# A ConvNeXt block on one core: normalised rows on three of every four partitions, read in three transfers

## The chip, the cores and the metric

The kernel runs on one core of a Trainium2 chip. A core has TensorE (PE; its weight loads are shown as PEld), VectorE (DVE), ScalarE (ACT), GpSimd (POOL) and SyncE (SP), which here issues transfers and does no arithmetic, and 16 DMA engines that all queues share. SyncE's transfers go through one hardware queue, GpSimd's through a software queue. The metric is the device time of one execution in microseconds (us).

## The reference

The input is one image of 512 x 512 pixels with 96 channels in bf16. The block is a depthwise 3 x 3 convolution, a layer norm over the channels, a linear layer from 96 to 384, gelu, a global response norm, a linear layer back to 96 and a residual:

```python
    for i in range(K):
        for j in range(K):
            out = out + xp[:, i:i+H, j:j+W, :] * dw[i, j][None, None, None, :]
    h = _layernorm(out, axis=-1)
    h = jnp.einsum('bhwc,ce->bhwe', h, w1)
    h = _gelu(h)
    gx = jnp.sqrt((h * h).sum(axis=(1, 2), keepdims=True) + 1e-6)
    nx = gx / (gx.mean(axis=-1, keepdims=True) + 1e-6)
    h = grn_gamma * (h * nx) + grn_beta + h
    h = jnp.einsum('bhwe,ec->bhwc', h, w2)
    return x + h
```

The response norm needs, for each of the 384 hidden channels, the sum of squares of gelu's output over the whole image. No pixel of the output can be made before the last pixel of h has been summed. So the work falls into two phases.

## The kernel before

The image is cut into 128 blocks of 4 rows (2,048 pixels). **Phase 1** goes through slots, one block of convolution in each. A block's input is loaded by SyncE (`load_x`, tile xin), turned by DVE so that channels lie on partitions (`turn_x`, xT), convolved on PE as matmuls with diagonal weights, and copied to SBUF by ACT (y_bf). A partition of y_bf holds one channel of one image row: partition 32r + c has row r and channels 3c, 3c+1, 3c+2 of the kernel's own order in its three sections. GpSimd squares it (`stage_sq`, ysq), PE sums y and ysq over the channels (`stage_stats`), and the statistics of a batch of four blocks become 1/std on GpSimd (`stage_rstd`, `stage_newton`). These are transposed by DVE (rt), written to DRAM by SyncE (`stage_rows`, r_dram) and read back as a broadcast over 32 partitions in four transfers (`stage_bcast`, tile rbc). GpSimd multiplies y by it (`stage_norm`, tile yn). The mean is taken off by the weights: w1p is w1 minus its mean over the channels.

The layout of yn is not what the linear layer needs (all 96 channels on partitions, for all 2,048 pixels of a block). So `stage_write` writes yn to DRAM in four transfers of 32 partitions (96 KB each), into `yn_dram[block]`, 96 rows of 2,048 pixels, 4 KB a row, and `stage_read` reads the 96 rows back into one of the six tiles of `yn_ring` (ynT). Row k goes to partition k. Partitions 96 to 127 of each ring tile are set to zero once, and so are rows 96 to 127 of w1p, so matmuls contract over 128 partitions.

Two slots after the read, `mlp_units` (or `mlp_tail` in the last 14 blocks) multiplies ynT by w1p on PE, ACT applies gelu (tile g), and sums of squares are taken either by DVE (bn_stats, bst) or by PE (matmuls of g with itself). For blocks whose number ends in 0, 3 or 7 ("whole"), up to the last 14, g is stored to g_dram in three parts.

All of phase 1 is in program order on each engine; the order in which the functions are called is the order in each queue. In a slot SyncE's queue holds: the next x block, the ynT read, the four writes of yn, the four broadcasts or the two transfers of rows where it is their turn in the batch, and one part of a g store. The read of a block waits for that block's write, issued one slot earlier. GpSimd's queue holds in a slot: the newton steps, yn, ysq, the rstd steps.

**Phase 2** goes over the 128 blocks in ORDER. 35 whole blocks are loaded from g_dram by GpSimd's queue (tile gl, 1.5 MB each); five blocks are still held in SBUF; for the other 88 g is made again from yn (tile gr): `load_rest` reads the block's rows into a ring tile five blocks ahead, except for the three blocks in KEPT, whose tiles are still there. This read takes 128 rows, the block's 96 and the first 32 of the next block, 512 KB; the 32 extra rows meet the zero rows of w1p. For every block, x is loaded a second time (`load_xr`, xr), GpSimd adds a bias to it (xb), PE multiplies g by the scaled w2, DVE adds xb to the result (o_sb, four buffers), and SyncE stores it (`stage_out`) after the next block's matmuls have been queued. A tile of o_sb is free again once its store has landed.

Setup: w1 is loaded by ACT's queue in three transfers of 32 rows, to partitions i, i+3, i+6 and so on, so that its rows have the order of yn_dram's. `setup_mlp` sums w1 over the channels with a matmul by ones (cen) and forms w1p. `setup_ynt` clears the ring's padding on GpSimd in the first slot.

Most calls go through a helper that records the program order, so L35 is the line of most instructions.

Of the kernel before, what the change touches and what calls it, by code (L numbers as in the profile page):

```python
# [12 lines left out]
GR = 4  # L13
# [43 lines left out]
def kernel(  # L57
# [11 lines left out]
    f32 = mybir.dt.float32  # L69
    i32 = mybir.dt.int32  # L70
    bf16 = x.dtype
    assert bf16 == mybir.dt.bfloat16

    B, H, W, C = x.shape
    E = w1.shape[1]
    assert B == 1 and dw.shape[0] == 3 and dw.shape[1] == 3
    assert C == 96 and E % 128 == 0 and W == 512
    NI = C // 32
# [8 lines left out]
    yn_dram = dram.tile([NBLK, C, GR * W], bf16, name="yn_dram")  # L87
# [6 lines left out]
    def is_held(q):  # L94
        return q in HELD

    def is_whole(q):
        return q < TAIL0 and q % 10 in WHOLE
# [11 lines left out]
    def chans(i):  # L110
        return slice(i, 64, 2) if i < 2 else slice(64, 96)
# [8 lines left out]
        return flat_ap.rearrange("p (g r m) -> p g r m", r=GR, m=MB)  # L120

    def yn_src(q):
        return yn_dram[q].rearrange("c (r w) -> c r w", r=GR)

    def yn_rows(q):
        return yn_dram[q:q + 2].rearrange("q c (r w) -> (q c) r w", r=GR)[0:128]

    def yn_dst(q, r):
        return yn_dram[q].rearrange("(c i) (r w) -> r c i w", i=NI, r=GR)[r]
# [1 line left out]
    consts = ctx.enter_context(tc.tile_pool(name="consts", bufs=1))  # L131
# [4 lines left out]
    dwx = consts.tile([9, NI, GR, 32], bf16, name="dwx")  # L136
    eye32 = consts.tile([128, 32], bf16, name="eye32")
    rowsel = consts.tile([128, GR], bf16, name="rowsel")
    w1_raw = consts.tile([C, E], bf16, name="w1_raw")
    w1p = consts.tile([128, E], bf16, name="w1p")  # L140
    Wq = consts.tile([128, NI, 3, GR, 32], bf16, name="Wq")
    w2_sb = consts.tile([128, NCH, C], bf16, name="w2_sb")
# [41 lines left out]
    with ExitStack() as p1:  # L184
        pe, dve, act, pool, sp = (InOrder(tc, e) for e in (nc.tensor, nc.vector, nc.scalar, nc.gpsimd, nc.sync))
# [3 lines left out]
        def banks(n):  # L189
            if n == 2:  # L190
                return PS[:, 0:2, :]
            ones[0] += 1
            return PS[:, 2 + ones[0] % 2:3 + ones[0] % 2, :]
# [48 lines left out]
        for b in range(min(2, NBLK)):  # L242
# [3 lines left out]
                       in_=zrow[:, None, :NI * GR * 32].to_broadcast([128, 3, NI * GR * 32]), func=ACTF.Identity)  # L246
# [4 lines left out]
        for q in range(GR):  # L251
            dve.tensor_copy(out=eye32[32 * q:32 * q + 32, :], in_=ident_f[32 * q:32 * q + 32, 32 * q:32 * q + 32])

        cen = consts.tile([C, 128], bf16, name="cen")
        xtpool = pc.enter_context(tc.tile_pool(name="xt", side="right", bufs=1))
        ypool = pc.enter_context(tc.tile_pool(name="ybf", side="right", bufs=13))
        ysqpool = pc.enter_context(tc.tile_pool(name="ysq", side="right", bufs=3))
# [25 lines left out]
        def load_rest(n, sq, pq):  # L283
            q = ORDER[n]
            v = grp.setdefault(q, {})
            if is_held(q):
                v["g"] = gs[q]
            elif is_whole(q):
                v["g"] = late.gl.tile([128, NQ, NCH, QW], bf16, name="gl")
                pq.dma_start(out=v["g"][:].rearrange("p t j w -> p (t j w)"), in_=g_dram[whole.index(q)])  # L290
            else:
                ynt = yn_ring[SLOTS[nth_made[q] % NYT]]
                if q not in KEPT:
                    sq.dma_start(out=ynt[:], in_=yn_rows(q))
                v["ynt"] = ynt

        def recompute(q, t):
# [87 lines left out]
        for j in range(GR):  # L385
            pool.memset(rowsel[32 * j:32 * j + 32, j:j + 1], 1.0)
        pool.memset(cen[:], 1.0)
        pool.memset(w1p[C:128, :], 0.0)
        dve.memset(SG, 0.0)
        busy(FILL[0])  # L390
        Ud = banks(2)[:, 0, :NI * 9].rearrange("p (i k) -> p i k", i=NI)
# [4 lines left out]
        for i in range(NI):  # L396
            dve.tensor_tensor(out=Wd[:, i], in0=eye32[:, None, :].to_broadcast([128, 9, 32]),
                              in1=Ud[:, i, :, None].to_broadcast([128, 9, 32]), op=ALU.mult)
# [13 lines left out]
                            pool.tensor_copy(out=o, in_=i_)  # L412

        for i in range(NI):
            act.dma_start(out=w1_raw[i:C:NI, :], in_=w1[chans(i), :])
        act.dma_start(out=w2_sb[:], in_=w2.rearrange("(j p) c -> p j c", p=128))
        with nc.allow_non_contiguous_dma("tiny gamma/beta load"):
            act.dma_start(out=gam_bf[:], in_=grn_gamma.rearrange("(j p) -> p j", p=128))
# [1 line left out]

        def setup_ynt():
            for t in yn_ring:
                pool.memset(t[C:128, :, :].rearrange("p r w -> p (r w)").bitcast(f32), 0.0)

        def setup_mlp():
            Us = banks(1)[:, 0, :]
            w1m, b2_ps = Us[:, :E], Us[:, E:E + C]
            pe.matmul(w1m, lhsT=cen[:], rhs=w1_raw[:], start=True, stop=True)
            for j in range(NCH):
                pe.matmul(b2_ps, lhsT=bet_bf[:, j:j + 1].to_broadcast([128, 128]), rhs=w2_sb[:, j, :],  # L430
                          start=(j == 0), stop=(j == NCH - 1))
            dve.scalar_tensor_tensor(out=w1p[:C, :], in0=w1m[:C], scalar=-1.0 / C, in1=w1_raw[:],
                                     op0=ALU.mult, op1=ALU.add)
            dve.tensor_copy(out=B2bc_f[:], in_=b2_ps)

# [210 lines left out]

        def stage_read(b):
            t = yn_ring[b % NYT]
            sp.dma_start(out=t[:C], in_=yn_src(b))
            ynts[b] = t  # L650

        bsts = {}
# [173 lines left out]
        for s in range(last_slot + 1):  # L826
# [3 lines left out]
            for b in get("read"):  # L830
                stage_read(b)
# [53 lines left out]
            else:  # L885
                b = mlp[0]
# [38 lines left out]
            if s == 0:  # L925
                setup_ynt()
            if s == 3:
                setup_mlp()
# [18 lines left out]
            if s == last_slot:  # L947
                for n in range(PRE):
                    load_rest(n, sp, sp)
# [19 lines left out]
        r = gi[:].bitcast(f32)  # L969
        for it in range(3):  # L970
# [5 lines left out]
            r = rn_[:]  # L976
# [21 lines left out]
    with p2:  # L998
        def out_part(q, o_sb, sub):
            r0 = q * GR  # L1000
            nc.sync.dma_start(
                out=out[0, r0:r0 + GR].rearrange("r w c -> (r w) c").rearrange(
                    "(p g) c -> p g c", g=PXP)[:, sub * GPS:(sub + 1) * GPS],
                in_=o_sb[:, sub * GPS:(sub + 1) * GPS])

        held = None
        FIRST = 8
        for n, q in enumerate(ORDER):
            sq, pq = (sp, pool) if n < FIRST else (nc.sync, nc.gpsimd)
            if n + PRE < NBLK:  # L1010
                load_rest(n + PRE, sq, pq)
                load_xr(n + PRE, pq)
            if 3 <= n + 2 < NBLK:
                stage_xb(ORDER[n + 2], pq, B2c)
            if n == NBLK - 1:
                stage_out(*held)
                held = None
            o_sb = stage_mm2(n, q)
            if held:
                stage_out(*held)  # L1020
            held = (q, o_sb)
# [30 lines left out]
```

## Time and profile before

| | |
|---|---|
| runs | 1481.22 us median of 3 (1476.22 to 1484.95) |
| profiled execution | span 1480.8 us; no other time of this execution is given |
| PE busy | 1391.3 us (94%) |
| ACT busy | 1414.4 us (96%) |
| POOL busy | 1300.3 us (88%) |
| DVE busy | 1182.0 us (80%) |
| granted TensorE clock | 0.994 |
| moved by DMA | 433.08 MB, 292 GB/s over the span |
| ynT reads, phase 1 | 128 of 384 KB |
| ynT reads, phase 2 | 85 of 512 KB |

The page gives busy time by engine, a strip of 40 slices, the DMA queues, the chain of work that ended last, the costliest groups of instructions with what ended the idle time before them, and the DMA issues. Further views give the same by stretch of time, the waits by pair of engines, and the timeline of one engine. "SPq" is SyncE's queue; its issues are not counted as busy time. In a timeline line the first number is the start from the span's beginning, the second the duration of the merged instructions, xN how many were merged, and the bracket is idle time before them and what ended it.

### The profile page before, as it was taken

The numbers are of one execution on the slowest core, as the hardware profiler recorded it, in microseconds if no ns is written. First come the engines' busy times: TensorE is split into PE (matmuls) and PEld (weight loads), VectorE is DVE, ScalarE is ACT, GpSimd is POOL, SyncE is SP. The second block draws the span as 40 slices with busy tenths as digits, with TensorE's granted clock in tenths as the row PEclk, the third lists the DMA queues.
The fourth block names the chain that finished last, engine by engine and source line by source line (L and its number), as shares of the span: only waits on it lengthen the run. The fifth ranks groups of instructions, "written<-read, shape, count | busy, mean of one in ns | idle before, by whom it ended". The sixth has DMA issues, their size and how long they took to land.

```text
span 1480.8 us, 54225 instructions
## 1 busy us (share of the span) xinstructions
PE 1391.3 (94%) x23125; PEld 810.4 (55%) x23125; DVE 1182.0 (80%) x2135; ACT 1414.4 (96%) x1595; POOL 1300.3 (88%) x922
## 2 busy tenths in 40 slices
PE   8888999999999999999999997789999999999998
PEld 3434444444444444444444445467777777776776
DVE  7849989999999999999999987965555555555555
ACT  7888989999999999999999999999999999999997
POOL 3459889998998999998999987569999999999997
PEclk9999999999999999999999999999999999999999
DMA  5568788788888888888888866669999999999997
GB/s 180 179 205 255 241 253 280 228 271 260 260 248 264 258 264 255 276 253 254 263 258 266 263 216 195 195 225 409 366 359 402 417 416 413 419 410 417 411 412 282
DMA packets 167768, 433.08 MB, mean 292 GB/s; under 512 B 31558, under 2 KB 81318, under 8 KB 163046
## 3 DMA queue, kind: packets, MB, share of 16 engines
q1 hardware_dynamic: 151284, 326.04, 66.3%
q0 software_dynamic: 14880, 103.43, 17.6%
q8 instruction: 181, 2.97, 0.8%
q14 instruction: 61, 0.50, 0.1%
q10 hardware_dynamic: 1362, 0.15, 0.1%
HBM read 273.30 MB, written 156.22 MB: 290 GB/s over the span
## 4 chain that ended last, share of the span: by engine, by line
PE 30%; ACT 24%; DMA 19%; POOL 13%; DVE 6%; issue 4%; SPq 4%; POOLq 0%; ACTq 0%; DVEq 0%
PE PS L35 30%; ACT g L35 16%; DMA out_dram<-o_sb 9%; POOL yn L35 6%; ACT y_bf L35 5%; POOL ysq L35 5%; SPq L35 4%; DMA yn_dram<-yn 3%; DVE bst L35 3%; DMA xin<-in_x_dram 2%; DMA rbc<-r_dram 2%; DMA ynT<-yn_dram 1%; DMA g_dram<-g 1%; DVE o_sb L35 1%; ACT xT L35 1%
## 5 line engine op out<-in xcount | busy, mean ns | idle before, releaser
L35 ACT ACTIVATE g<-PS 128x512 bf16<-128x512 f32 (+2 forms) x1062 | 727.7, 864 | 16.5 <-PE PS L35 15.6
L35 DVE BATCH_NORM_STATS2 bst<-g 128x6 f32<-128x512 bf16 x1110 | 671.3, 672 | 35.4 <-ACT g L35 34.5
L35 PE MATMUL PS<-ynT,w1p 128*128 128x512 bf16 x2181 | 609.6, 381 | 23.6 <-ACT g L35 5.4
L35 ACT ACTIVATE gr<-PS 128x1536 bf16<-128x1536 f32 x360 | 498.5, 1459 | 18.8 <-PE PS L35 13.8
L35 POOL TENSOR_TENSOR yn<-y_bf,rbc 128x1536 bf16<-128x1536 bf16 x126 | 391.3, 3108 | 77.3 <-ACT rbc L35 21.9
L35 DVE TENSOR_TENSOR o_sb<-PS,xb 128x384 bf16<-128x384 f32 x512 | 277.3, 556 | 227.0 <-PE PS L35 190.1
L324 POOL TENSOR_TENSOR xb<-xr,B2c 128x1536 f32<-128x1536 bf16 x118 | 368.1, 3133 | 4.3 <-DVE o_sb L35 2.0
L35 PE MATMUL PS<-xT,Wq 64*32 64x511 bf16 (+1 forms) x9198 | 340.5, 389 | 26.2 <-ACT y_bf L35 8.1
L35 POOL TENSOR_TENSOR ysq<-y_bf 128x1536 bf16<-128x1536 bf16 x114 | 313.6, 2752 | 12.8 <-ACT y_bf L35 12.8
L35 PEld LDWEIGHTS <-w1p 128*128 128x128 bf16 x2181 | 171.6, 98 | 222.0 <-issue 133.4
L35 PEld LDWEIGHTS <-gr 128*128 128x128 bf16 x4296 | 212.1, 98 | 68.9 <-issue 12.0
L35 PE MATMUL PS<-W2s,gr 128*128 128x96 bf16 x4224 | 223.5, 206 | 8.2 <-DVE o_sb L35 8.0
L35 PEld LDWEIGHTS <-Wq 64*32 64x32 bf16 x9216 | 111.9, 90 | 193.3 <-issue 145.9
L35 ACT ACTIVATE y_bf<-PS 128x1536 bf16<-128x1536 f32 (+2 forms) x135 | 199.4, 1482 | 17.4 <-PE PS L35 13.3
L35 DVE STREAM_TRANSPOSE xT<-xin 128x576 f32<-128x576 f32 (+1 forms) x256 | 181.4, 748 | 8.1 <-DMA xin<-in_x_dram 8.1
L35 PEld LDWEIGHTS <-g 128*128 128x128 bf16 x1704 | 104.9, 98 | 86.3 <-issue 54.3
L35 PE MATMUL PS<-w1p,ynT 128*128 128x256 bf16 (+2 forms) x822 | 125.8, 273 | 8.0 <-ACT xT L35 3.2
L35 PE MATMUL PS<-g 128*128 128x128 bf16 x1464 | 122.6, 220 | 2.9 <-DVE PS L35 2.6
L35 PEld LDWEIGHTS <-gl 128*128 128x128 bf16 x1680 | 82.8, 98 | 26.8 <-issue 5.0
L35 PE MATMUL PS<-W2s,gl 128*128 128x96 bf16 x1680 | 89.5, 206 | 3.4 <-DVE o_sb L35 3.2
L35 PEld LDWEIGHTS <-ynT 128*128 128x128 bf16 x822 | 64.1, 97 | 31.5 <-issue 13.7
L279 POOL DMA_DIRECT2D xr<-in_x_dram x115 | 63.7, 555 | 14.2 <-POOL xb L324 14.2
(105 smaller groups left out, 576.5 us busy)
## 6 DMA issues: line engine op xcount, KB each, us to landing
xin<-in_x_dram SPq DMA_DIRECT2D x126, 432.0 KB
g_dram<-g SPq DMA_DIRECT2D x105, 512.0 KB
gl<-g_dram POOLq DMA_DIRECT2D x35, 1536.0 KB, 11.3
yn_dram<-yn SPq DMA_DIRECT2D x512, 96.0 KB
ynT<-yn_dram SPq DMA_DIRECT2D x128, 384.0 KB
out_dram<-o_sb SPq DMA_DIRECT2D x127, 384.0 KB
xr<-in_x_dram POOLq DMA_DIRECT2D x123, 384.0 KB, 6.9
ynT<-yn_dram SPq DMA_DIRECT2D x85, 512.0 KB
```

What stands on the lines that cost most here:

```text
L35: r = f(*a, **k)
L279: pq.dma_start(out=xr[:], in_=x[0, r0:r0 + GR].rearrange("r w c -> (r w) c").rearrange("(p g) c -> p g c", g=PXP))
L324: pq.tensor_tensor(out=xb[:], in0=grp[q]["xr"][:], in1=bias[:, None, :].to_broadcast([128, PXP, C]), op=ALU.add)
```

## The change

Row 3c+i of a block's 96 rows goes to partition 4c+i, for c from 0 to 31 and i from 0 to 2. Every fourth partition (3, 7, 11 and so on to 127) holds zeros. This needs three transfers for each read, one for each i: 32 rows that lie 12 KB apart in DRAM, to partitions i, i+4, i+8 and so on, 128 KB each. Both phases read this way, on the same queue and at the same place in the program as the one transfer before. Phase 2 reads the 96 rows of its block alone. w1 is loaded to the same partitions, w1_raw, cen and w1p take all 128 partitions, and the memsets clear whole tiles: w1_raw in place of the last 32 rows of w1p, and the six ring tiles over 128 partitions instead of 32. The writes of yn are as before.

```diff
     def yn_src(q):
-        return yn_dram[q].rearrange("c (r w) -> c r w", r=GR)
-
-    def yn_rows(q):
-        return yn_dram[q:q + 2].rearrange("q c (r w) -> (q c) r w", r=GR)[0:128]
+        return yn_dram[q].rearrange("(c i) (r w) -> i c r w", i=NI, r=GR)
+
+    def read_yn(eng, t, q):
+        for i in range(NI):
+            eng.dma_start(out=t[i:128:4], in_=yn_src(q)[i])
...
-    w1_raw = consts.tile([C, E], bf16, name="w1_raw")
+    w1_raw = consts.tile([128, E], bf16, name="w1_raw")
...
-        cen = consts.tile([C, 128], bf16, name="cen")
+        cen = consts.tile([128, 128], bf16, name="cen")
...
                 if q not in KEPT:
-                    sq.dma_start(out=ynt[:], in_=yn_rows(q))
+                    read_yn(sq, ynt, q)
...
-        pool.memset(w1p[C:128, :], 0.0)
+        pool.memset(w1_raw[:], 0.0)
...
-            act.dma_start(out=w1_raw[i:C:NI, :], in_=w1[chans(i), :])
+            act.dma_start(out=w1_raw[i:128:4, :], in_=w1[chans(i), :])
...
-                pool.memset(t[C:128, :, :].rearrange("p r w -> p (r w)").bitcast(f32), 0.0)
+                pool.memset(t[:].rearrange("p r w -> p (r w)").bitcast(f32), 0.0)
...
-            dve.scalar_tensor_tensor(out=w1p[:C, :], in0=w1m[:C], scalar=-1.0 / C, in1=w1_raw[:],
+            dve.scalar_tensor_tensor(out=w1p[:], in0=w1m, scalar=-1.0 / C, in1=w1_raw[:],
                                      op0=ALU.mult, op1=ALU.add)
...
         def stage_read(b):
             t = yn_ring[b % NYT]
-            sp.dma_start(out=t[:C], in_=yn_src(b))
+            read_yn(sp, t, b)
             ynts[b] = t
```

## The prediction

> **What bounds the kernel now.** I read the busy time by stretch first, because the program has two phases with different limits: phase 1 runs to about 900 us, and phase 2 from about 1000 us.
>
> ```profile
> core 0: us, PE busy (x) PEld busy (x) DVE busy (x) ACT busy (x) POOL busy (x), PEclk, DMA share, GB/s
> 400.00:500.00 100.00, 95.87 (x1753) 47.05 (x1738) 99.55 (x171) 99.44 (x143) 93.38 (x71) 1.00 0.82 250
> ...
> 1050.00:1100.00 50.00, 50.00 (x740) 37.33 (x739) 28.34 (x53) 49.47 (x37) 47.12 (x29) 1.00 0.98 363
> 1100.00:1150.00 50.00, 50.00 (x735) 37.19 (x732) 28.38 (x53) 49.52 (x37) 48.38 (x30) 1.00 1.00 388
> ...
> 1200.00:1250.00 50.00, 48.19 (x704) 35.55 (x703) 26.95 (x51) 47.47 (x35) 48.37 (x31) 1.00 1.02 416
> ```
>
> The columns are the stretch, each engine's busy time and instructions, the granted clock (full throughout), the DMA share and rate. Phase 1 is ACT at 99%, and POOL's 93% hides little slack, as shown below. Phase 2 has two regimes. Up to 1142 us PE is never idle, at 363 to 388 GB/s. After that the DMA engines are full (1.02 at 411 to 417 GB/s) and PE does 708 matmuls per 50 us (mean of the six windows from 1150 to 1450) where it did 737. The waits of 1150 to 1450 say through what:
>
> ```profile
> DVE o_sb L35 <- DMA out_dram<-o_sb: 29.8, 20, 2.7
> ...
> PE PS L35 <- DVE o_sb L35: 9.3, 11, 1.6
> ```
>
> Stores land too late to free one of the four o_sb buffers, DVE stands, then PE. Second, SyncE's queue and POOL in one batch of phase 1 (timeline; start, duration):
>
> ```profile
> 405.03 2.49 SPq L35 DMA_DIRECT2D yn_dram<-yn  x4
> 407.56 1.17 SPq L35 DMA_DIRECT2D r_dram<-rt  x2
> 408.83 0.41 SPq L35 DMA_DIRECT2D g_dram<-g  x1
> 409.29 0.43 SPq L35 DMA_DIRECT2D xin<-in_x_dram  x1
> 409.90 0.59 SPq L35 DMA_DIRECT2D ynT<-yn_dram  x1
> 410.80 3.27 SPq L35 DMA_DIRECT2D yn_dram<-yn  x4
> 414.11 2.32 SPq L35 DMA_DIRECT2D rbc<-r_dram  x4
> ```
> ```profile
> 401.89 3.11 POOL L35 TENSOR_TENSOR yn<-y_bf,rbc 128x1536 bf16<-128x1536 bf16 x1
> ...
> 416.49 2.76 POOL L35 TENSOR_TENSOR ysq<-y_bf 128x1536 bf16<-128x1536 bf16 x1
> 419.88 3.11 POOL L35 TENSOR_TENSOR yn<-y_bf,rbc 128x1536 bf16<-128x1536 bf16 x1 [0.63 <-DMA xin<-in_x_dram]
> ```
>
> Here is a loop. POOL ends a yn at 405.0; SyncE at once issues its write, then rows, store, x, the ynT read, the next write and the rbc broadcast, nearly without a gap, until 416.4. The broadcast lands some 3.4 us later, and POOL, which has gone through ysq, yn, ysq, yn, ysq, stands 0.63 us for it. In 20 of the 26 batches from 200 us on, POOL has such a wait at this place (0.4 to 5.9 us). Does POOL's delay reach the end? It does through ysq, which PE needs for the sums. The slack from a ysq's end to PE's use of it (two timelines, matched block by block from block 127 back) is 5.4 us at block 34, 3.7 at 46, 1.0 at 54 and 0.06 at blocks 70, 74, 82, 98 and 126, where PE stands:
>
> ```profile
> 693.47 0.46 PE L35 MATMUL PS<-rowsel,ysq 128*128 128x4 bf16 x12 [2.01 <-POOL ysq L35]
> ```
>
> So from about block 54 POOL, ACT and SyncE's chain go at one pace (28.15 us for a batch of four), and a longer chain is paid for.
>
> **The change part by part.**
>
> *Phase 2 reads 384 KB, not 512 KB.* 85 reads save 128 KB each, 11.1 MB; 50 of them lie between 1150 and 1450, where they are 6.6 MB of 124 MB (413.8 GB/s x 300 us). What can be won is the stall: PE at 737 per 50 us would need 288 us for that stretch, 12 us less; 1.5 us (PE's idle time at 1000 to 1050) come on top. So the bounds are 0 and 13.5 us. At full pace the stretch would need 117.5 MB in 288 us, 408 GB/s: above the 388 that ran without a stall, below the 414 moved when saturated. That is on the edge, so some bursts will still stall; I take 8 us. Below nothing: two more issues ahead of each store delay it by up to 1.2 us, but the read is issued 1.1 us or more before the store's own data is ready (SyncE waited 339.6 us for DVE's o_sb in 127 waits), so I bound that loss at 3 us.
>
> *One read becomes three issues on SyncE.* The price of one more issue: a ynT read after an idle moment takes 0.325 us (median). The nearest row in shape is the w1 load: 32 rows to every third partition, back to back.
>
> ```profile
> L35 ACTq DMA_DIRECT2D w_raw<-in_w_dram x3: 593/594/602, 5.6 to 6.9; - x3
> ```
>
> The broadcast's issues, 32 rows of 4 KB, took 0.50 to 0.58 in most batches. I take 0.55, so 1.1 us per block; bounds 2 x 0.32 and 2 x 0.6. Only the first of the three can wait for the write's landing, a wait that exists already. Queued behind them on SyncE are the next write, the rows and the broadcast. In the loop above one read lies between POOL's yn and the broadcast, so rbc lands 1.1 us later; mostly the write follows its read at once (0.04 to 0.07 us), in six batches 0.25 to 0.8 us of idle time takes part of it, 0.1 on the mean. With 20 of 26 batches paying the full 1.0 and the others about 0.3: 0.8 us of POOL per batch. POOL's slack now falls by 0.6 us per batch (5.4 to 0.06 over nine); at 1.4 it is gone four batches after block 34, at block 50. The 19 batches from there to 126 pay 0.8 each, **15 us**. Bounds: 0.35 per batch (cheap issues, and the gain of the next part) is 7 us; for above see the rivals.
>
> *Rows over all 128 partitions in phase 1.* The 4 KB packets of the trace have a median of 159 ns in both phases, but a mean of 199 from 200 to 800 us against 161 from 1150 to 1450, where the reads already fill 128 partitions. If the 96-row reads cause it, six packets per engine lose 40 ns each: at most 0.24 us of a landing. Nothing waits for that read: it is issued 10 to 15 us ahead of its matmul. I count zero, and use the 0.24 in the low bound only.
>
> *The ramp.* Between 83 and 118 us the chain runs through SyncE and POOL with two reads in it (89.16, 96.63): 2 us; bounds 0 and 4.
>
> *Semaphores, memsets, w1.* Two more completions per read and engine, 9 ns each in the trace: 18 ns x 85 = 1.5 us of DMA time over phase 2, inside the edge above. The memsets go over 128 partitions with the same length per partition (six of 0.95 us, done at 12.2; the first read comes at 25.8). The w1_raw memset stands where w1p's did (over at 2.8; w1 is loaded from 5.6). The weight sum's matmul (0.33 us, once) takes 128 rows for 96. All zero; without that cover the memsets would cost 6 us once. Phase 1's matmuls have a contraction of 128 already.
>
> *Sum* against the profiled span: 1480.8 + 15 + 2 - 8 = **1490 us**. The median of the runs, 1481.22, stands 0.4 above that span, so I add nothing around it.
>
> [...]
>
> **The rivals.**
>
> *A, the other side: the issues are hidden.* SyncE idles 173 of the 600 us. If the two issues cost 0.32 each and rbc lands sooner by 0.24, the 0.35 left per batch may find POOL's small waits shrinking elsewhere; decisive is that POOL's slack at blocks 50 to 126 stays above zero. Then phase 2's gain decides: with all of PE's 10.9 us of idle time (9.4 + 1.5) gone and the ramp's 2, **1472**. Against it: the zeros at 70 to 126.
>
> *B, SyncE becomes the bound of phase 1.* From 200 to 800 it has 427 us of issues and 82.8 of landing waits; 84 blocks x 1.1 make it 602 of 600. If it enters the batch late, a second set lies in the loop: 1.9 per batch, slack gone at block 42, 21 batches x 1.7 = 36 us: 1480.8 + 36 + 2 - 8 = **1511**. For it: in the three quick blocks of a batch POOL makes a yn every 5.8 us. Against it: POOL's pause of 10 us before the next batch lets SyncE catch up.
>
> *C, phase 2 wins nothing* (the reads give way to the other loads and the stores stay late, or three small transfers drain worse): **1498**.
>
> **How the numbers follow.** Chances: forecast 0.5, A 0.2, B 0.13, C 0.17. The forecast's own range is 1482 to 1498 (phase 1 at its low bound of 7 us at one end, nothing won in phase 2 at the other). The 8-in-10 range reaches from A to just short of B: 1472 to 1508. A change within 0.5% (1473.8 to 1488.6) can hardly be told from none. Faster: two thirds of A, 0.14. Same: the rest of A and the forecast's low two fifths, 0.27. Slower: 0.59.
>
> **What would show it.** Right: the ynT reads of phase 1 as groups of three at 0.5 to 0.6 us; longer POOL waits ahead of yn; more PE waits for ysq; ACT below 99% from 500 to 900; phase 1 longer by 15 us; in phase 2 PE nearer 737 per 50 us and DVE's wait for out_dram well under 35 us. Wrong: issues of 0.3 us, unchanged POOL waits (A); SyncE busy with hardly a wait (B); DVE's wait for out_dram unchanged (C).

## The result and the profile after

The changed kernel takes 1542.15 us in the median (1533.4 to 1547.18), the kernel before 1481.83 us. The ratio is 1.0417, with a 95% interval of 1.0385 to 1.0449. The forecast was 1490 us, in a range of 1472 to 1508: right in direction, far too small in size. The profiled execution is the shortest of the changed kernel's, with a span of 1531.6 us. So the traces account for 50.8 us (1531.6 - 1480.8) of some 60.

Where they lie is read from three moments: the start of the last y_bf (the last convolution's copy), the start of the first o_sb (phase 2 begins) and of the last o_sb. The tile's view has first and last start, before and changed:

```profile
L35 DVE TENSOR_TENSOR o_sb<-PS,xb x512: 545/557/559, 975.5 to 1477.4; 128x384 bf16<-128x384 f32 x171
```
```profile
L35 DVE TENSOR_TENSOR o_sb<-PS,xb x512: 547/558/559, 1031.0 to 1528.3; 128x384 bf16<-128x384 f32 x171
```

| | before | changed | difference |
|---|---|---|---|
| last y_bf | 883.7 | 928.8 | +45.1 |
| first o_sb | 975.5 | 1031.0 | +55.5 |
| first to last o_sb | 501.9 | 497.3 | -4.6 |

Phase 2 became shorter, by about half of what was forecast. All of the loss lies in phase 1: 45 us while blocks are convolved, and 10 us behind the last convolution, where the queue still carries reads and writes of yn and PE waits 8.3 us for ynT. The busy time by stretch shows both sides (columns as in the profile before: stretch, engines with their instructions, clock, DMA share, GB/s):

```profile
400.00:500.00 100.00, 91.31 (x1637) 44.66 (x1636) 93.73 (x161) 94.35 (x135) 87.94 (x63) 0.98 0.77 245
...
1250.00:1300.00 50.00, 49.24 (x720) 36.37 (x717) 27.65 (x51) 48.64 (x37) 48.38 (x29) 1.00 1.01 398
1300.00:1350.00 50.00, 49.20 (x720) 36.33 (x718) 27.60 (x51) 48.51 (x36) 48.67 (x31) 1.00 1.01 393
```

In phase 1 every engine that computes is less busy: ACT 94 us of 100 for 99, POOL 88 for 93, and DMA has a lower share, 0.77 for 0.82. The granted clock is lower too, 0.98 for 1.00; more on it below. Something that is not on this list holds them. SyncE's queue in one batch (timeline: start, duration, merged issues) shows what, beside GpSimd:

```profile
635.13 0.39 SPq L35 DMA_DIRECT2D xin<-in_x_dram  x1
636.14 1.77 SPq L35 DMA_DIRECT2D ynT<-yn_dram  x3
637.95 3.37 SPq L35 DMA_DIRECT2D yn_dram<-yn  x4
641.42 1.17 SPq L35 DMA_DIRECT2D r_dram<-rt  x2
642.70 0.41 SPq L35 DMA_DIRECT2D g_dram<-g  x1
643.15 0.43 SPq L35 DMA_DIRECT2D xin<-in_x_dram  x1
643.76 1.89 SPq L35 DMA_DIRECT2D ynT<-yn_dram  x3
645.70 3.05 SPq L35 DMA_DIRECT2D yn_dram<-yn  x4
648.79 1.99 SPq L35 DMA_DIRECT2D rbc<-r_dram  x4
```
```profile
633.44 3.10 POOL L35 TENSOR_TENSOR yn<-y_bf,rbc 128x1536 bf16<-128x1536 bf16 x1
...
639.20 3.10 POOL L35 TENSOR_TENSOR yn<-y_bf,rbc 128x1536 bf16<-128x1536 bf16 x1
...
653.32 3.11 POOL L35 TENSOR_TENSOR yn<-y_bf,rbc 128x1536 bf16<-128x1536 bf16 x1 [2.53 <-DMA rbc<-r_dram]
```

The first yn is done at 636.5 and its write starts at 637.95; the second is done at 642.3 and its write starts 3.4 us later, at 645.70. In the batch shown of before, the second write started as soon as its yn was done, at 410.80:

```profile
407.67 3.10 POOL L35 TENSOR_TENSOR yn<-y_bf,rbc 128x1536 bf16<-128x1536 bf16 x1
```

SyncE is hardly anywhere ahead of GpSimd now: its waits for yn from 200 to 800 us were 38.0 us in 24 times before and are now (SyncE's own waits)

```profile
SPq L35 <- POOL yn L35: 1.0, 2, 0.5
```

In these 600 us SyncE's issues take 510 us (the sum of their own times), for 417 before, while fewer blocks pass: 238 read issues in threes, 79 blocks, for 84. Its pauses of more than 0.3 us between two issues shrink from 144 us to 44. The lateness goes where the prediction followed it. GpSimd waits for rbc, its ysq comes late, and PE stands. The first line is before, from 200 to 800 us, the second the changed kernel in the same stretch:

```profile
PE PS L35 <- POOL ysq L35: 3.4, 3, 2.0
```
```profile
PE PS L35 <- POOL ysq L35: 25.1, 15, 3.2
```

Behind this wait the trace has one more step, which the prediction had at nothing. One such wait, and the stretch that follows (columns as above):

```profile
517.93 0.48 PE L35 MATMUL PS<-rowsel,ysq 128*128 128x4 bf16 x12 [2.58 <-POOL ysq L35]
```
```profile
517.40:524.20 6.80, 6.04 (x68) 1.73 (x69) 4.94 (x9) 2.38 (x4) 6.80 (x4) 0.50 0.71 208
524.20:530.00 5.80, 5.57 (x106) 2.91 (x112) 5.49 (x11) 5.74 (x9) 5.20 (x2) 1.00 0.83 259
```

The granted clock is 0.50 for 6.8 us. PE hardly pauses, but does 68 matmuls in this time, and ACT, phase 1's fullest engine, is busy for only 2.4 us of it. From 200 to 800 us the changed kernel has seven such stretches of 3.4 or 6.8 us, 34.1 us in all, each begun during a PE wait of 1.4 to 3.2 us for ysq or within 1.6 us of its end; the kernel before has one of 3.4 us, behind the 2.01 us wait that the prediction shows. ACT is idle for 34.5 us of these 600 us, for 4.2 before, and 22.7 of the 34.5 lie in the seven stretches. That the wait lowers the clock is read from their order in time; no run keeps the clock up through such a wait, and two waits of 1.6 and 1.8 us passed without a drop.

In phase 2 the waits of 1150 to 1450 us changed their kind as forecast. DVE's wait for out_dram, 29.8 us before, is all but gone; one for GpSimd's xb stands in its place:

```profile
DVE o_sb L35 <- POOL xb L325: 27.0, 36, 1.5
...
PE PS L35 <- DVE o_sb L35: 3.2, 10, 0.4
DVE o_sb L35 <- DMA out_dram<-o_sb: 1.5, 1, 1.5
```

### The profile page after: what moved, and what is told of

Same layout as the page of the kernel before. It is cut to its first block, busy times and chain, and to the rows that moved or that the text cites. A ratio compares the mean times of both kernels' runs of the same rounds, so it can differ in the third digit from the quotient of the medians.

```text
span 1531.6 us, 54859 instructions
## 1 busy us (share of the span) xinstructions
PE 1405.8 (92%) x23125; PEld 816.0 (53%) x23125; DVE 1194.2 (78%) x2135; ACT 1422.4 (93%) x1595; POOL 1299.3 (85%) x922
## 4 chain that ended last, share of the span: by engine, by line
PE 26%; POOL 23%; DMA 10%; ACT 10%; SPq 8%; issue 4%; DVE 3%; POOLq 0%; ACTq 0%; DVEq 0%
PE PS L35 26%; POOL xb L325 10%; SPq L35 8%; ACT g L35 7%; POOL ysq L35 5%; POOL yn L35 5%; DMA yn_dram<-yn 4%; DMA rbc<-r_dram 2%; DMA ynT<-yn_dram 2%; ACT y_bf L35 2%; DMA xin<-in_x_dram 1%; DVE bst L35 1%; POOL xr L280 1%; POOL var L35 1%; POOL nt L35 1%
## 5 line engine op out<-in xcount | busy, mean ns | idle before, releaser
L35 PE MATMUL PS<-xT,Wq 64*32 64x511 bf16 (+1 forms) x9198 | 348.4, 397 | 18.4 <-ACT y_bf L35 4.9
L35 ACT ACTIVATE y_bf<-PS 128x1536 bf16<-128x1536 f32 (+2 forms) x135 | 192.3, 1430 | 16.0 <-PE PS L35 11.5
L35 PE MATMUL PS<-rowsel,ysq 128*128 128x4 bf16 x1536 | 57.1, 166 | 38.9 <-POOL ysq L35 37.9
```

Source lines behind the costliest of these rows:

```text
L35: r = f(*a, **k)
```

## The experiments

Theory 1 was that the two additional issues on SyncE's queue make the loss. The rivals were the layout (rows 12 KB apart, every fourth partition), the data arriving in three transfers, and the place of the reads in the queue against the queue's time as a whole. "First o_sb" is compared with 975.5 us of the kernel before throughout, and "phase 2" is first to last o_sb, 501.9 us there. Each kernel has one trace: two kernels below whose phase 1 is that of the kernel before have their first o_sb at 970.4 and 972.4, so some 5 us say nothing.

**The split alone.** Phase 1's read in three, over the old partitions:

```diff
-            sp.dma_start(out=t[:C], in_=yn_src(b))
+            for i in range(NI):
+                sp.dma_start(out=t[32 * i:32 * i + 32], in_=yn_src(b)[32 * i:32 * i + 32])
```

> The kernel before with one edit in phase 1: the read is split into three transfers of 32 rows, to partitions 0 to 31, 32 to 63 and 64 to 95 as before, rows contiguous in DRAM. Theory 1 (it is the number of issues on SyncE's queue): the three take 1.8 to 2.1 us a block, GpSimd waits for rbc as in the changed kernel, the first o_sb comes 45 to 60 us later than before, time 1525 to 1540 us. Rival (it is the layout: rows 12 KB apart, every fourth partition): 1480 to 1490.

1524.05 us, ratio 1.0293 (1.0248 to 1.0338); first o_sb at 1017.0, 41.5 us later, and phase 2 unchanged at 504.2. So three quarters of phase 1's loss (41.5 of 55.5 us) needs neither the new partitions nor the new rows. The issues took 0.48 to 0.51 us each, less than expected and less than the 0.64 to 0.67 us of the changed kernel. That difference had to be found.

**Two issues that carry next to nothing.** The read stays whole; behind it stand two transfers of 32 rows of 64 bytes:

```diff
             sp.dma_start(out=t[:C], in_=yn_src(b))
+            for i in range(2):
+                sp.dma_start(out=spare_t[:, i, :], in_=x[0, 0, 0:32, 0:32])
```

> The kernel before with two small transfers added on SyncE behind each read of phase 1 (32 rows of 64 bytes of x into a tile that nobody reads); the read itself is not split. Theory (the issues alone make the loss): 0.5 to 0.6 us for each, first o_sb 35 to 50 us later, time 1512 to 1530 us. Rival (the loss comes from the read's data being in three transfers, each with its own completion): 1478 to 1485.

1519.71 us, ratio 1.0267 (1.0218 to 1.0315); first o_sb at 1016.7, 41.2 us later, at 0.47 to 0.50 us for each added issue. The same loss with 4 KB a block added and no read split: the issues make it, not the data.

**One additional issue.** Two transfers of 48 rows:

```diff
-            sp.dma_start(out=t[:C], in_=yn_src(b))
+            for h in range(2):
+                sp.dma_start(out=t[48 * h:48 * h + 48], in_=yn_src(b)[48 * h:48 * h + 48])
```

> The kernel before with phase 1's read split into two transfers of 48 rows: one more issue, some 0.5 us a block, where the split into three of 32 rows added two and made the first o_sb 41 us later. Theory (SyncE has slack of about 0.6 us a block and becomes the bound beyond it): the first issue fits into the slack, the first o_sb is 0 to 8 us later, time 1475 to 1490 us. Rival (every issue counts alike): half of the split's loss, 1498 to 1504 us.

1496.9 us, ratio 1.0101 (1.0052 to 1.015). The time lies between the two expectations. The table has the issue time of the reads (and added transfers) of a block from 200 to 800 us, the first o_sb, the mean time of a batch of four blocks (start of ysq, block 28 to block 124), and the median's distance from that of the kernel before, run beside it:

| | issue time a block | added | first o_sb later by | batch | median later by |
|---|---|---|---|---|---|
| before | 0.45 us | | | 28.5 us | |
| two of 48 rows | 1.06 us | 0.61 us | 10.8 us | 28.9 us | 17.3 us |
| two small ones added | 1.51 us | 1.06 us | 41.2 us | 29.7 us | 40.1 us |
| three, old partitions | 1.49 us | 1.04 us | 41.5 us | 29.9 us | 46.4 us |
| changed kernel | 1.97 us | 1.52 us | 55.5 us | 30.25 us | 60.3 us |

The one issue costs a quarter of the split's loss by the trace, and some two fifths by the medians, where a proportional rule asks for half. So some slack is likely, but its size is not shown. Nor is the added time paid in full: the split adds 4.2 us of issue time to a batch, which gets 1.4 us longer; the changed kernel adds 6.1, and its batch gets 1.75 us longer.

**Which stride is dear.** First the changed kernel with each transfer's rows next to each other in DRAM, still to every fourth partition; then the kernel with the split alone, over contiguous partitions, with rows 12 KB apart (its edit is shown against that kernel):

```diff
-        return yn_dram[q].rearrange("(c i) (r w) -> i c r w", i=NI, r=GR)
+        return yn_dram[q].rearrange("(i c) (r w) -> i c r w", i=NI, r=GR)
```

> The changed kernel, but the 32 rows of each transfer lie next to each other in DRAM; they still go to every fourth partition. The weights are not put in the order that this needs, so the output is not the reference's; the work is the same. It shows which of the two strides makes an issue 0.65 us where the split over contiguous partitions took 0.50. If it is the partitions: 0.64 to 0.67 us, phase 1 as in the changed kernel, 1535 to 1547 us. If it is the rows 12 KB apart: 0.48 to 0.52 us, some 14 us less, 1520 to 1532 us.

```diff
-                sp.dma_start(out=t[32 * i:32 * i + 32], in_=yn_src(b)[32 * i:32 * i + 32])
+                sp.dma_start(out=t[32 * i:32 * i + 32], in_=yn_dram[b].rearrange("(c i) (r w) -> i c r w", i=NI, r=GR)[i])
```

> The split of phase 1's read into three over contiguous partitions, but each takes every third row of DRAM (12 KB apart). The weights are not put in the order that this needs, so the output is not the reference's; the work is the same. If the stride of the rows makes an issue dear: 0.64 to 0.67 us and a time of 1535 to 1542 us. If not: 0.48 to 0.52 us and 1520 to 1528 us as with contiguous rows.

The tile's own view gives the issue's shortest, median and longest time in ns, first for the strided partitions, then for the strided rows:

```profile
L35 SPq DMA_DIRECT2D ynT<-yn_dram x402: 447/587/2054, 26.4 to 1054.4; - x134
```
```profile
L35 SPq DMA_DIRECT2D ynT<-yn_dram x390: 302/419/2336, 26.2 to 1033.8; - x195
```

The split over contiguous partitions and rows has 302 and 419 as well, the changed kernel 447 and 587. So it is the partitions: an issue to every fourth partition takes SyncE 0.145 us more at the shortest and 0.168 in the median, and rows 12 KB apart cost nothing. The times follow: 1533.46 us (first o_sb 1033.3) and 1523.53 us (1014.1).

**The reads moved out of the loop.** The changed kernel, with the reads of a slot behind the writes, broadcasts, rows and stores instead of ahead of them:

```diff
-            for b in get("read"):
-                stage_read(b)
             for b in get("write"):
...
             store_next()
+            for b in get("read"):
+                stage_read(b)
```

> The changed kernel with its three reads moved, in each slot of phase 1, from ahead of the write of yn to the end of SyncE's slot, behind the broadcasts, rows and stores. All issues stay. Theory 1 (the reads lie in the loop from GpSimd's yn through SyncE to rbc): the loop loses them and the wait for the write's landing, GpSimd's wait for rbc falls under 20 us, phase 1 is back at ACT's pace, time 1473 to 1485 us. Rival (SyncE is short of time as a whole, wherever the issues stand): 1510 to 1540.

1507.28 us, ratio 1.0194 (1.0156 to 1.0231): between the two again. First o_sb comes at 1007.3, so 24 of the 55.5 us come back and 32 do not. SyncE's timeline says why:

```profile
606.50 2.58 SPq L35 DMA_DIRECT2D yn_dram<-yn  x4
609.13 2.56 SPq L35 DMA_DIRECT2D rbc<-r_dram  x4
611.79 0.37 SPq L35 DMA_DIRECT2D g_dram<-g  x1
612.26 1.96 SPq L35 DMA_DIRECT2D ynT<-yn_dram  x3
614.27 0.58 SPq L35 DMA_DIRECT2D xin<-in_x_dram  x1
614.95 3.07 SPq L35 DMA_DIRECT2D yn_dram<-yn  x4
618.11 0.53 SPq L35 DMA_DIRECT2D g_dram<-g  x1
618.74 2.02 SPq L35 DMA_DIRECT2D ynT<-yn_dram  x3
```

Every issue starts within 0.1 us of the end of the one ahead. From 200 to 800 us SyncE's issues take 536 us, and its pauses over 0.3 us come to 9. SyncE's wait for the landing of yn's writes, 82.8 us before and 28.8 in the changed kernel, is gone, and the queue is full. So both expectations held in part. The place of the reads costs 24 us, most likely through the landing that a read ahead of the write waits for while everything behind it stands; that part is argued. The other 32 are not the full queue's alone: 8 of them are lost by block 28, whose ysq starts at 195.9 us for 187.9, as in the next experiment (196.2), whose queue is not full. From there on a batch takes 29.45 us, for 28.5 before and 30.25 in the changed kernel.

**The kernel before with its one read late.** The same move on the kernel before.

> The kernel before with its one read moved in the same way to the end of SyncE's slot. Theory 1: GpSimd's waits for rbc (some 60 us over the run with those at the start) shrink and PE's waits for ysq vanish, but ACT was busy at 99% in phase 1 already, so the time is 1470 to 1481 us. Rival (the place of a single read does not matter): 1481.

1483.45 us, ratio 1.0039 (1.0015 to 1.0064), a little slower. PE's waits for ysq fell to 1.0 us over the whole run, as expected, and it won nothing, since ACT was at 99% in phase 1 already. PE gained a wait instead: 12.9 us for ynT, all but some 3 us of it in the first 200 us, where a late read has no two slots to spare.

**Phase 2's bytes alone.** The kernel before, whose phase 2 reads 96 rows to the lower 96 partitions:

```diff
-                    sq.dma_start(out=ynt[:], in_=yn_rows(q))
+                    sq.dma_start(out=ynt[:C], in_=yn_src(q))
```

> The kernel before with one edit in phase 2: the read takes the block's 96 rows to partitions 0 to 95 in one transfer, 384 KB for 512 KB; phase 1 is untouched. Theory 1 (saved bytes free the stores, GpSimd's xb is the next limit at 3.9 us a block): DVE's wait for out_dram falls from 35 us to under 10, a wait for POOL xb of 20 to 40 us takes its place, time 1473 to 1478 us. Rival (the saved bytes count in full): PE goes at 737 per 50 us to the end, time 1468 to 1471. Rival (96 rows on the lower partitions drain as slowly as 128): 1481.

None of the three: 1496.75 us, ratio 1.0138 (1.009 to 1.0186). Phase 2 takes 522.6 us, 20.7 more, with a quarter fewer bytes in these reads. The stretches, and the waits of 1150 to 1450 us:

```profile
1200.00:1250.00 50.00, 44.68 (x645) 32.58 (x644) 24.92 (x47) 43.71 (x32) 44.15 (x27) 1.00 1.02 372
1250.00:1300.00 50.00, 45.05 (x655) 33.02 (x652) 24.81 (x46) 45.91 (x34) 46.28 (x29) 1.00 1.02 375
```
```profile
DVE o_sb L35 <- DMA out_dram<-o_sb: 55.5, 31, 4.8
```

The DMA engines are as full as before (1.02) and move 372 to 375 GB/s where they moved 416. The 4 KB packets of these reads take 190 ns on the mean for 161 before (1150 to 1450 us); in the changed kernel, with the same 384 KB to three of every four partitions, they take 167 ns. Why they take longer to the lower 96 partitions is not shown. So the 128-row read of the kernel before is not waste: with it phase 2 took 501.9 us, without it 522.6. That the spread is what lets the changed kernel profit from fewer bytes is likely, not shown: its reads also come in three transfers, and no run has three transfers to the lower partitions in phase 2. In phase 1 the split alone had a mean 4 KB packet of 206 ns (199 before), split and spread together one of 190.

**Each phase with its own order.** Phase 1 as before, phase 2 as in the changed kernel, with a second w1p, w1q, in phase 2's order (made by one matmul with a permutation); read_spread is the three transfers to every fourth partition:

```diff
-                    sq.dma_start(out=ynt[:], in_=yn_rows(q))
+                    read_spread(sq, ynt, q)
...
-            cm_unit(grp[q]["g"], grp[q]["ynt"], t)
+            cm_unit(grp[q]["g"], grp[q]["ynt"], t, w1p if q in KEPT else w1q)
```

> Phase 1 as in the kernel before (one read of 96 rows to partitions 0 to 95), phase 2 as in the changed kernel (three reads of 32 rows to three of every four partitions), with a second copy of w1p in the order of phase 2. Theory (the loss is all in phase 1's queue, and phase 2 gains by bytes that are spread over all partitions): first o_sb at 975 to 980 us as before, phase 2 some 500 us, time 1472 to 1479 us. Rival (phase 2's gain in the changed kernel hangs on something of its phase 1): 1480 to 1500.

1478.15 us, ratio 0.9989 (0.9967 to 1.0011). First o_sb at 972.4, phase 2 497.5 us: in the trace the whole loss of phase 1 is gone and phase 2's gain is kept. But as a time it can't be told from the kernel before. With phase 1's read moved late from slot 40 on as well, the result is the same:

> One read of 96 rows in phase 1, three spread reads in phase 2 (two orders of w1p), and from slot 40 on phase 1's read moved to the end of SyncE's slot; the early slots, where the late read made PE wait 12.9 us for ynT, keep the old order. Theory (phase 1 at ACT's pace, GpSimd's waits for rbc less): 1468 to 1476 us. Rival (nothing to win in phase 1 where ACT is busy 99.9%): 1476 to 1480, as with the two orders alone.

1476.06 us, ratio 0.9998 (0.9982 to 1.0014). The rival held; no version here beats the kernel before by more than the measurement can tell.

**What holds the changed kernel's phase 2.** First its second loads of x moved from GpSimd's queue to SyncE's:

```diff
-                load_xr(n + PRE, pq)
+                load_xr(n + PRE, sq)
```

> The changed kernel with phase 2's loads of x for the residual issued by SyncE instead of GpSimd. Theory (in the changed kernel's phase 2 GpSimd's 3.13 us of xb and 0.55 us of issue a block are the bound): DVE's wait for POOL xb, 39 us there, falls under 5, phase 2 takes 485 to 495 us for 500.6, time 1528 to 1538 us. Rival (the DMA engines are the bound at a share of 1.01): 1540 to 1550.

1562.37 us, ratio 1.0538 (1.0478 to 1.0597), and phase 2 took 525.3 us: worse than either expectation. The wait for xb went, but GpSimd now waits for x and DVE for the stores again (1200 to 1500 us):

```profile
DVE o_sb L35 <- DMA out_dram<-o_sb: 41.0, 17, 4.3
...
POOL xb L325 <- DMA xr<-in_x_dram: 29.9, 12, 4.2
```

The DMA engines run at a share of 0.99 with only 356 to 371 GB/s. The loads come as 3 KB packets there, where GpSimd's queue made 6 KB ones, and they stand in one queue with the stores. Which of the two costs more was not tried. Then GpSimd's addition was left out altogether; tile xr, which DVE now reads, got eight buffers for five:

```diff
-            xb = late.xb.tile([128, PXP, C], f32, name="xb")
-            pq.tensor_tensor(out=xb[:], in0=grp[q]["xr"][:],
-                                    in1=bias[:, None, :].to_broadcast([128, PXP, C]), op=ALU.add)
-            grp[q]["xb"] = xb
+            grp[q]["xb"] = grp[q]["xr"]
```

> The changed kernel without GpSimd's xb in phase 2: DVE adds x itself, and the constant from beta and w2 is left out of the output; xr has eight buffers for five. The queues and the transfers stay as they are. Theory (with the stores' waits gone, GpSimd's 3.13 us of xb and 0.55 us of issue a block hold phase 2): DVE's 39 us of waiting for POOL xb end, PE keeps 737 matmuls per 50 us to the end, the first to the last o_sb takes 480 to 490 us for 497 in the changed kernel, time 1525 to 1535 us. Rival (the DMA engines hold it, at a share of 1.01): the waits go back to out_dram or to x, 495 to 500 us and 1537 to 1545.

1534.74 us, and phase 2 takes 496.9 us for 497.3. The theory fell: GpSimd was 80% idle there and nothing was won. The wait named last, xb, was not the limit. The DMA engines, at 1.00 to 1.02 from 1200 to 1500 us in both, are the reading that is left; the run doesn't isolate them, since a buffer of xr is now held until DVE is done with it, and GpSimd waits 175.0 us for that in these 300 us before it issues the next loads.

## Why the prediction was wrong

**What bounds the kernel now**: right. The saturated DMA of phase 2 and the loop from GpSimd through SyncE to rbc and back are both there, and in the changed kernel the loss reaches PE through ysq as described, with PE's waits from about block 30 on, for block 70 before. The granted clock of 0.50 that comes during or behind seven of PE's nine waits of 1.4 us or more (changed kernel, 200 to 800 us) is missing.

**"One read becomes three issues on SyncE", its price**: too low. I took 0.55 us for an added issue, between the broadcasts and the w1 loads. Measured were 0.64 to 0.67 us, and the first of the three became as dear as the others, so SyncE has 1.5 us more a block and not 1.1. The nearer row was in view: w1's loads to every third partition, 0.594 us. It was probably dear because of its strided partitions, and I averaged that away with a row that has none. But the price alone is not what failed: the split has 1.04 us a block, my own 1.1, and still lost 41.5 us.

**The same step, what a batch pays**: this is the failed step. I charged one set of reads per batch, where a read lies between GpSimd's yn and the broadcast, and only from block 50 on: 0.8 us in each of 19 batches, 15 us in all. Measured are 1.75 us per batch in all 24 batches from block 28 to 124 (30.25 for 28.50 us), 42 us, and at my own price, in the split, 1.4 us, 34 us.

Two things stand in the charge's place. First, SyncE is late already when the loop begins. In the batch shown two sets of reads lie between the first yn and the broadcast, the rest of one (to 637.91) and all of the other (643.76 to 645.65); in a batch of the split the first write still starts at once (yn done at 600.5, write at 600.49). That is rival B's mechanism, which I gave 0.13 because GpSimd's pause before the next batch would let SyncE catch up; its 1.7 us per batch is near what was measured, and its 1511 us is still too low.

Second, I let a late ysq cost its own lateness and nothing more. In the trace the clock is at 0.50 during or behind those seven waits, for 34.1 us in all, and 22.7 of ACT's 34.5 idle us from 200 to 800 us lie there (15.5 of 28.0 in the split). The other 11.8 us, over the 20 batches of that stretch, are 0.6 us a batch, near my 0.8. So the term that I put at nothing may be most of the miss; how much of these 22.7 us would be lost at full clock stays open.

My sum for B, 427 + 83 + 92 = 602 of 600 us, does not measure the room either. With the split's 1.04 us it is 597, just fitting, and the split lost 41.5 us; and the 83 us of landing waits did not stay, they were 28.8 in the changed kernel.

**The ramp, the last blocks**: I had 2 us for the ramp, which the traces can't tell from none: block 28's ysq starts at 191.2 us for 187.9, and at 191.2 as well in the kernel whose phase 1 is as before and whose phase 2 is the changed one. I had nothing for the last blocks. Between the last y_bf and the first o_sb 10 us were lost (102.2 us for 91.8), where the queue carries the same sets; with the reads moved late this stretch was back at 92.0.

**Phase 2 reads 384 KB**: right in sign and mechanism, 4.6 us for 8. The rate fell together with the bytes, from 414 GB/s to 391 in 1150 to 1450 us at nearly the same share (1.02 and 1.01), so the forecast's 408 needed was not on offer. That 384 KB to the 96 lower partitions would have lost 20.7 us instead, the prediction didn't see; the experiment shows it.

**Rows over all partitions in phase 1**: counted as zero. No run tried the spread there with one issue, so it stays open. The mean 4 KB packet fell from 199 ns only to 190, so most of its distance from phase 2's 161 stayed; at a DMA share of 0.83 there was little for it to win.

**An issue's cost and its bytes**: two issues that moved 4 KB a block, at 0.47 to 0.50 us each, cost 41 us, on a queue whose issues and landing waits already took some 500 of 600 us (417 and 82.8).

Some 10 us of the median's loss lie outside the profiled execution, which was the shortest; where they arise isn't shown.

## What to carry to other kernels

Add up the issuing queue as one adds up an engine: the time of its issues plus the landing waits inside its program order, against the period of the stage. Here the sum was 500 of 600 us, and two further issues a block made the first o_sb 41 us later though they moved only 4 KB; how much a further issue costs, the sum does not tell. Follow a delay to the engine that bounds the stage, and look there at the granted clock: here a PE that stood for 2 us or more mostly (25 of 30 waits) went on at a clock of 0.50 for another 3.4 or 6.8 us. Price an issue by a row with the same stride over partitions: here it took 0.587 us in the median to every fourth partition and 0.419 to contiguous ones. And count bytes by the partitions that they reach: here reads of 384 KB to the lower 96 partitions made phase 2 20.7 us longer than reads of 512 KB to all 128.

## What was not expected of the hardware

- From 200 to 800 us the fourteen traces have 48 stretches of 3.4 or 6.8 us at a granted TensorE clock of 0.50, the kernel before one of them and the changed kernel seven. Every one begins during a wait of PE of at least 1.3 us or within 2.5 us of its end, and 25 of the 30 waits of 2 us or more have one.
- An issue on SyncE to every fourth partition took at least 0.447 us and 0.587 in the median, to contiguous partitions 0.302 and 0.419, for the same 32 rows; with rows 12 KB apart in DRAM, to contiguous partitions, it was 0.302 and 0.419 again.
- The same reads with 384 KB to partitions 0 to 95 instead of 512 KB to all 128 lowered the rate of the whole core's DMA from 416 to 372 GB/s at a share of 1.02, and lengthened phase 2 by 20.7 us.
- Loads of x moved from GpSimd's queue to SyncE's came as 3 KB packets instead of 6 KB, and phase 2 became 28 us longer.
